# Another place modulo 512 bytes in SBUF for the activations of each chunk: windowed attention and a two-layer FFN on one core

## The chip, the cores and the metric

The kernel runs on one core of one Trainium2 chip. A core has five engines that run side by side: TensorE (PE: matmuls and transposes, results in PSUM; the loading of a matmul's stationary operand is shown apart as PEld), VectorE (DVE), ScalarE (ACT), GpSimd (POOL) and SyncE (SP, which here issues the DMAs). SBUF is the working memory on the chip, with 128 partitions; an address below is a byte address within a partition. The metric is the device time of the program in microseconds.

## The reference, cut to what matters

```python
# attention, batch 4, heads 8, seq 768, head_dim 64
k_sum = k.reshape(B, H, 24, 32, D).max(axis=3)
v_sum = v.reshape(B, H, 24, 32, D).mean(axis=3)
scores_l = scale * (q @ k.T)          # kept where |i - j| < 16
scores_s = scale * (q @ k_sum.T) + log(32)
a = softmax(concat(scores_l masked, scores_s))
attn = a @ concat(v, v_sum)
# feed-forward, 3072 tokens, d_model 512, d_ff 2048
x = attn.transpose(0, 2, 1, 3).reshape(3072, 512)
r = maximum(x @ w_in, 0)
out = (s * r * r + b) @ w_out
```

## The kernel before

The 3,072 tokens are worked on in 12 chunks of 256, c = 0 to 11 (three per batch entry); "chunk" below always counts from 0. For each chunk the attention of 4 pairs of heads gives x, kept transposed as 4 blocks (kc) of 128 features by 256 tokens. The feed-forward part then runs over 16 slices f of 128 hidden features:

- `hidden` (L364 in the trace) makes ph, 128 hidden features by 256 tokens: the stationary operand is a 128x128 block of w_in, the streamed one is x[:, kc], 256 columns. In chunks 1 to 11 the operands are split into a high and a low part (xh, xl and wh, wl, of type fp32r), and the sum has three products, w_l xh, w_h xl and w_h xh, over four kc: 12 matmuls per f, 192 per chunk. Chunk 0 uses plain fp32: 4 matmuls of the code per f, each of which is two instructions in the trace.
- `activate` makes g = s r^2 + b from ph: ACT (relu, square), POOL (scale and shift, L382), then DVE writes gh (L384) and gl (L386).
- `project` (L401) adds to po: the stationary operand is a block of 128 tokens of gh or gl, the streamed one is w_out (wh, wl), 512 columns. Two blocks of tokens by three products: 6 matmuls per f, 96 per chunk.
- `evict` copies po out and stores it.

So in `hidden` the activations are streamed and the weights are loaded, and in `project` it is the other way round. The weights of the next matmul are loaded while the present one streams.

The order of the work is written out by hand: `at(step, order, fn, ...)` files every piece under a step, two steps of f at a time; `project` of f comes two steps behind `activate` (LAG = 2), and the attention of chunk c + 1 (scores L266, transposes L314, values L334) is spread over the steps of chunk c. In chunk 11 there is no attention left to do.

Tiles come from pools, and a pool places its tiles one after the other. Weights lie in the pools `slots` and `wring`, whose tiles are 4,096 and 2,048 bytes; x, xh, xl, r, g, gh and gl are tags of the pool `p2`. In the built program of before every weight tile begins at 128 modulo 512, and every xh, xl, gh and gl of every chunk at 320 modulo 512, so that the two are 192 bytes apart in that measure. The blocks inside the tiles are 512, 1,024 or 2,048 bytes apart, so all operands of the fp32r matmuls begin at these two values.

Of the kernel before, what the change touches and what calls it, by code (L numbers as in the profile page):

```python
# [10 lines left out]
F32 = mybir.dt.float32  # L11
F32R = mybir.dt.float32r
# [6 lines left out]
P = 128  # L19
# [9 lines left out]
T = NSUB * SUB  # L29
# [4 lines left out]
NKC = DM // P  # L34
# [10 lines left out]
def windowed_attention_then_relu2_ffn(ctx, tc, qk, vwin, kt, vt, kq, vrow, wp, sb, out):  # L45


    nc = tc.nc
# [5 lines left out]
    p2 = ctx.enter_context(tc.tile_pool(name="p2", bufs=2))  # L54
# [160 lines left out]
    qk_t, vw_t, ps_of, pr_of, mn_of, sm_of, pt_of, pT_of, o_of, xt = ({} for _ in range(10))  # L215
# [107 lines left out]
    def values(c, p):  # L323
# [8 lines left out]
        for i in range(NSUB):  # L332
            for e in range(2):
# [2 lines left out]
                    vw[:, e, i, :], pT[:, e * T + i * SUB : e * T + (i + 1) * SUB], start=True, stop=True,  # L336
                )

    def attended(c, p):
        if p == 0:  # L340
            if c == 0:
                xt[c] = (p2.tile([P, NKC, T], F32, name="x", tag="xh"),)
            else:
                xt[c] = p2.tile([P, NKC, T], F32R, name="xh", tag="xh"), p2.tile([P, NKC, T], F32R, name="xl")
        kcs = slice(p, p + (1 if c < 2 else 2))
        o = o_of.pop((c, p))[:, : (kcs.stop - p) * T].rearrange("p (k t) -> p k t", t=T)
        nc.scalar.copy(xt[c][0][:, kcs], o)
        if c > 0:
            nc.vector.tensor_tensor(xt[c][1][:, kcs], o, xt[c][0][:, kcs].bitcast(F32), ALU.subtract)
# [18 lines left out]
    def activate(c, f):  # L368
        ph = ph_of.pop((c, f))
        r = p2.tile([P, T], F32, name="r")  # L370
        nc.scalar.activation(r, ph, AF.Relu)  # L371
        nc.scalar.activation(r, r, AF.Square)  # L372
        if c == 0:
            g = p2.tile([P, T], F32, name="g0", tag="gh", bufs=4)
            if f < 2:
                nc.vector.tensor_scalar(g, r, s_col, b_col, ALU.mult, ALU.add)
            else:
                nc.scalar.activation(g, r, AF.Identity, bias=b_col, scale=s_col)  # L378
            gg[c, f] = (g,)
            return  # L380
        g = p2.tile([P, T], F32, name="g")
        nc.gpsimd.tensor_scalar(g, r, s_col, b_col, ALU.mult, ALU.add)  # L382
        gh = p2.tile([P, T], F32R, name="gh", tag="gh", bufs=4)
        nc.vector.tensor_copy(gh, g)  # L384
        gl = p2.tile([P, T], F32R, name="gl", bufs=4)
        nc.vector.tensor_tensor(gl, g, gh.bitcast(F32), ALU.subtract)  # L386
        gg[c, f] = gh, gl

# [61 lines left out]
    for c in range(1, NC):  # L450
        bi, ci = place(c)
        for p in range(NPAIR):
# [31 lines left out]
            if c < 2 or p % 2 == 0:  # L484
                at(xa, ATT, attended, c, p)
# [10 lines left out]
    for i in range(NC * NF):  # L496
        c, f = divmod(i, NF)

        at(i if c == 0 else i - i % 2, HID, hidden, c, f)
        at(i, CHAIN, activate, c, f)  # L500
        at(i + LAG if i + LAG < NF else (i + LAG) | 1, PROJ, project, c, f)
        if f == NF - 1:
            at((i + LAG) | 1, EVICT, evict, c)
# [59 lines left out]
```

## Time and profile before

| what | value |
|---|---|
| median of two runs | 649.12 us (649.11 to 649.12) |
| the profiled execution | 648.77 us |
| its span, from the first to the last instruction | 647.1 us |
| mean granted clock of TensorE | 0.997 |
| HBM read and written | 55.90 MB, 6.29 MB |

The most expensive groups of TensorE on the page:

```profile
L401 PE MATMUL po<-wh,gl 128*128 128x512 f32 x352 | 143.2, 407 | 0.0
L364 PE MATMUL ph<-xh,wl_in 128*128 128x256 f32 x704 | 110.9, 280 | 0.0
L364 PEld LDWEIGHTS ph<-xh,wl_in 128*128 128x128 f32 x704 | 100.2, 188 | 8.2 <-ACT r L372 0.5
```

A row gives line, engine, operation, result and operands, shape and count; behind the first bar the busy time in us and the mean duration of one in ns, behind the second the idle time of the engine just before. Matmuls are pipelined: one that is recorded with 407 ns begins while the one before it is still under way, so that what a matmul costs in a row of them is read from start to start.

### The profile page before, as it was taken

The numbers are of one execution on the slowest core, as the hardware profiler recorded it, in microseconds if no ns is written. First come the engines' busy times: TensorE is split into PE (matmuls) and PEld (weight loads), VectorE is DVE, ScalarE is ACT, GpSimd is POOL, SyncE is SP. The second block draws the span as 40 slices with busy tenths as digits, with TensorE's granted clock in tenths as the row PEclk, the third lists the DMA queues.
The fourth block names the chain that finished last, engine by engine and source line by source line (L and its number), as shares of the span: only waits on it lengthen the run. The fifth ranks groups of instructions, "written<-read, shape, count | busy, mean of one in ns | idle before, by whom it ended". The sixth has DMA issues, their size and how long they took to land.

```text
span 647.1 us, 13906 instructions
## 1 busy us (share of the span) xinstructions
PE 630.3 (97%) x5164; PEld 549.1 (85%) x5164; DVE 332.7 (51%) x1088; ACT 338.4 (52%) x986; POOL 153.8 (24%) x324
## 2 busy tenths in 40 slices
PE   6799999999999999999999999999999999999997
PEld 4566568989989899898999899898998989999996
DVE  5799988885443434356434434447443353342221
ACT  4899998845444435535435345444444444452322
POOL 3000004143133132232231331331322322312221
PEclk9999999999999999999999999999999999999999
DMA  9999405035203204124402301504420320100000
GB/s 323 386 383 355 131 1 187 1 102 191 72 1 104 72 2 139 49 84 141 141 1 63 115 2 34 153 23 132 146 66 2 105 72 2 57 3 1 33 2 33
DMA packets 25604, 63.25 MB, mean 98 GB/s; under 512 B 3968, under 2 KB 3968, under 8 KB 25536
## 3 DMA queue, kind: packets, MB, share of 16 engines
q1 hardware_dynamic: 25536, 62.36, 29.3%
q8 instruction: 41, 0.67, 0.4%
q14 instruction: 27, 0.22, 0.1%
HBM read 55.90 MB, written 6.29 MB: 96 GB/s over the span
## 4 chain that ended last, share of the span: by engine, by line
PE 86%; ACT 7%; DMA 4%; DVE 2%; issue 0%; SPq 0%; DVEq 0%
PE po L401 39%; PE ph L364 38%; PE pav L334 4%; PE ps L266 3%; PE pt L314 3%; DMA wraw<-in_wp_dram 3%; ACT wraw L116 2%; ACT wraw L117 2%; ACT g L378 1%; DMA kq<-in_kq_dram 1%; ACT pr L298 1%; ACT r L372 1%; ACT r L371 0%; DVE wf_out L134 0%; DVE wf_out L132 0%; DVE wf_in L132 0%
## 5 line engine op out<-in xcount | busy, mean ns | idle before, releaser
L382 POOL TENSOR_SCALAR g<-r,sb_col 128x256 f32<-128x256 f32 x176 | 101.7, 578 | 418.5 <-ACT r L372 322.0
L384 DVE CAST gh<-g 128x256 fp32r<-128x256 f32 x176 | 52.4, 298 | 269.9 <-POOL g L382 269.6
L371 ACT ACTIVATE r<-ph 128x256 f32<-128x256 f32 x192 | 73.4, 382 | 203.8 <-PE ph L364 203.2
L401 PE MATMUL po<-wh,gl 128*128 128x512 f32 x352 | 143.2, 407 | 0.0
L401 PE MATMUL po<-wh,gh 128*128 128x512 f32 x352 | 138.6, 394 | 0.0
L401 PE MATMUL po<-wl_out,gh 128*128 128x512 f32 x352 | 137.7, 391 | 0.0
L364 PE MATMUL ph<-xh,wl_in 128*128 128x256 f32 x704 | 110.9, 280 | 0.0
L364 PE MATMUL ph<-xl,wh 128*128 128x256 f32 x704 | 108.7, 276 | 0.0
L364 PE MATMUL ph<-xh,wh 128*128 128x256 f32 x704 | 108.7, 276 | 0.0
L364 PEld LDWEIGHTS ph<-xh,wl_in 128*128 128x128 f32 x704 | 100.2, 188 | 8.2 <-ACT r L372 0.5
L364 PEld LDWEIGHTS ph<-xl,wh 128*128 128x128 f32 x704 | 93.8, 188 | 0.0
L364 PEld LDWEIGHTS ph<-xh,wh 128*128 128x128 f32 x704 | 92.9, 188 | 0.0
L372 ACT ACTIVATE r<-r 128x256 f32<-128x256 f32 x192 | 80.4, 419 | 6.1
L386 DVE TENSOR_TENSOR gl<-g,gh 128x256 fp32r<-128x256 f32 x176 | 76.4, 434 | 6.0
L401 PEld LDWEIGHTS po<-wh,gh 128*128 128x128 f32 x352 | 66.1, 188 | 14.3
L401 PEld LDWEIGHTS po<-wh,gl 128*128 128x128 f32 x352 | 66.2, 188 | 14.1 <-issue 3.0
L401 PEld LDWEIGHTS po<-wl_out,gh 128*128 128x128 f32 x352 | 66.3, 188 | 11.5
L298 ACT ACTIVATE pr<-pr,mn 128x120 f32<-128x120 f32 x176 | 67.4, 386 | 3.5 <-DVE mn L285 3.3
L321 ACT COPY pT<-pt 120x512 f32<-120x512 f32 x48 | 28.2, 587 | 37.0 <-PE pt L314 36.8
L364 PEld LDWEIGHTS ph<-x,wf_in 128*128 128x128 f32 x128 | 25.0, 200 | 14.3 <-issue 2.6
L244 POOL COPY vw<-vsum 24x256 f32<-24x256 f32 x80 | 36.8, 500 | 1.3
L308 DVE TENSOR_TENSOR pr<-pr,rs 128x480 f32<-128x480 f32 x48 | 35.4, 737 | 1.7
(71 smaller groups left out, 615.6 us busy)
## 6 DMA issues: line engine op xcount, KB each, us to landing
wraw<-in_wp_dram SPq DMA_DIRECT2D x32, 512.0 KB, 10.0
qk<-in_qk_dram SPq DMA_DIRECT2D x44, 368.0 KB, 4.7
vw<-in_vwin_dram SPq DMA_DIRECT2D x48, 192.0 KB, 4.2
out_dram<-o SPq DMA_DIRECT2D x24, 256.0 KB, 2.0
kraw<-in_kt_dram SPq DMA_DIRECT2D x12, 384.0 KB, 3.4
vraw<-in_vt_dram SPq DMA_DIRECT2D x12, 252.0 KB, 4.7
kq<-in_kq_dram SPq DMA_DIRECT2D x4, 512.0 KB, 4.6
vraw<-in_vt_dram SPq DMA_DIRECT2D x6, 264.0 KB, 7.0
```

The source lines that it names most:

```text
L244: filler(c).tensor_copy(vw_t[c, p][WIN:KR, e], vsum[bi][WIN : WIN + NB, 2 * p + e, :].unsqueeze(1).to_broadcast([NB, NSUB, D]),)
L298: nc.scalar.activation(pr, pr, AF.Exp, bias=mn_of[c, p][:, n : n + 1], scale=-1.0, accum_out=sm_of[c, p][:, n : n + 1])
L308: nc.vector.tensor_tensor(pr, pr, rs.unsqueeze(2).to_broadcast([P, 4, KR]), ALU.mult)
L321: nc.scalar.copy(pT_of[c, p], pt_of.pop((c, p))[:KR])
L334: nc.tensor.matmul(o[64 * e : 64 * e + 64, i * SUB : (i + 1) * SUB], vw[:, e, i, :], pT[:, e * T + i * SUB : e * T + (i + 1) * SUB], start ...
L364: nc.tensor.matmul(ph, w[:, kc * P : (kc + 1) * P], x[:, kc], start=(n == 0), stop=(n == len(terms) - 1))
L371: nc.scalar.activation(r, ph, AF.Relu)
L372: nc.scalar.activation(r, r, AF.Square)
L382: nc.gpsimd.tensor_scalar(g, r, s_col, b_col, ALU.mult, ALU.add)
L384: nc.vector.tensor_copy(gh, g)
L386: nc.vector.tensor_tensor(gl, g, gh.bitcast(F32), ALU.subtract)
L401: nc.tensor.matmul(po[t], a[:, t * P : (t + 1) * P], w, start=(f == 0 and n == 0), stop=(f == NF - 1 and n == len(terms) - 1),)
```

## The change

The tiles of xh, xl, gh and gl (and of x and g in chunk 0, which share their buffers) get 128 floats more, 512 bytes per block of buffers, and the kernel uses a part of them that begins `shift(c)` floats into the tile. Chunks 0 and 1 stay where they were, chunks 2 to 8 begin 64 bytes further modulo 512 with each chunk, and chunks 9, 10 and 11 lie at 32, 160 and 288 bytes from where chunk 1 lies. To make room, the scratch area for DMA descriptors at the start of SBUF is 2,048 bytes in place of 16,384.

```diff
+    def shift(c):
+
+        return 16 * (c - 1) if 1 <= c <= 8 else (0, 8, 40, 72)[c - 8] if c > 8 else 0
+
     def attended(c, p):
         if p == 0:
+            room = [P, NKC * T + 128]
             if c == 0:
-                xt[c] = (p2.tile([P, NKC, T], F32, name="x", tag="xh"),)
+                both = (p2.tile(room, F32, name="x", tag="xh"),)
             else:
-                xt[c] = p2.tile([P, NKC, T], F32R, name="xh", tag="xh"), p2.tile([P, NKC, T], F32R, name="xl")
+                both = p2.tile(room, F32R, name="xh", tag="xh"), p2.tile(room, F32R, name="xl")
+            xt[c] = [t[:, shift(c) : shift(c) + NKC * T].rearrange("p (k t) -> p k t", t=T) for t in both]
...
-            g = p2.tile([P, T], F32, name="g0", tag="gh", bufs=4)
+            g = p2.tile([P, T + 128], F32, name="g0", tag="gh", bufs=4)[:, :T]
...
-        gh = p2.tile([P, T], F32R, name="gh", tag="gh", bufs=4)
+        gh, gl = p2.tile([P, T + 128], F32R, name="gh", tag="gh", bufs=4), p2.tile([P, T + 128], F32R, name="gl", bufs=4)
+        gh, gl = gh[:, shift(c) : shift(c) + T], gl[:, shift(c) : shift(c) + T]
         nc.vector.tensor_copy(gh, g)
-        gl = p2.tile([P, T], F32R, name="gl", bufs=4)
...
-    nc = _bacc.Bacc("TRN2", target_bir_lowering=False, num_devices=1)
+    nc = _bacc.Bacc("TRN2", target_bir_lowering=False, num_devices=1, dynamic_dma_scratch_size=2048)
```

In the built program the instructions of every engine stand in the same order, with the same waits, as before. The operands lie so (bytes modulo 512; "distance" is the place of x and g minus that of the weights, modulo 512):

| chunk c | 0, 1 | 2 | 3 | 4 | 5 | 6 | 7 | 8 | 9 | 10 | 11 |
|---|---|---|---|---|---|---|---|---|---|---|---|
| x, g before | 320 | 320 | 320 | 320 | 320 | 320 | 320 | 320 | 320 | 320 | 320 |
| x, g after | 320 | 384 | 448 | 0 | 64 | 128 | 192 | 256 | 352 | 480 | 96 |
| weights, both | 128 | 128 | 128 | 128 | 128 | 128 | 128 | 128 | 128 | 128 | 128 |
| distance after | 192 | 256 | 320 | 384 | 448 | 0 | 64 | 128 | 224 | 352 | 480 |

All other tiles keep their place modulo 512; their addresses move by multiples of 512.

## The prediction

> **What bounds the kernel now.** I read the page's first parts, then the waits of TensorE, then windows cut at the chunks, then the order of time inside one chunk, and last the chain. The page:
>
> ```profile
> span 647.1 us, 13906 instructions
> PE 630.3 (97%) x5164; PEld 549.1 (85%) x5164; DVE 332.7 (51%) x1088; ACT 338.4 (52%) x986; POOL 153.8 (24%) x324
> PEclk9999999999999999999999999999999999999999
> ```
>
> PE is busy for 97% of the span, at the full granted clock in every slice. The waits of PE alone (who, for whom: total us, times, longest):
>
> ```profile
> PE ps L269 <- DMA kq<-in_kq_dram: 4.7, 1, 4.7
> PE ph L364 <- DVE wf_in L134: 2.7, 3, 1.9
> ...
> PE ps L270 <- DVE ksum L159: 0.4, 1, 0.4
> ```
>
> That is nine kinds of wait with about 13 us in all, and they lie ahead of the steady part. To see the steady part I cut windows at the first `hidden` matmul of c = 1, 2, ... 11 (window: its length, PE busy with its matmul count, clock, DMA share, GB/s):
>
> ```profile
> 99.33:150.79 51.46, 51.46 (x438) 1.00 0.36 104
> 150.79:201.08 50.29, 50.29 (x434) 1.00 0.22 72
> 201.08:251.37 50.29, 50.29 (x434) 1.00 0.17 58
> 251.37:301.67 50.30, 50.30 (x434) 1.00 0.35 107
> ...
> 502.84:553.14 50.30, 50.30 (x434) 1.00 0.18 58
> 553.14:602.47 49.33, 49.33 (x402) 1.00 0.06 20
> 602.47:647.07 44.60, 40.91 (x262) 1.00 0.07 24
> ```
>
> Two things are to be seen. PE never idles from chunk 1 to chunk 10. And the chunks 2 to 9 take the same 50.29 to 50.30 us, whatever the DMA does beside them (58 to 107 GB/s): in this stretch the time is the number of matmuls times the spacing of their starts, and nothing else. So only a change of that spacing can move the end.
>
> The spacing is read where no attention work lies between, in the last chunk (start us, us, engine line op, count of merged instructions):
>
> ```profile
> 632.23 0.39 PE L401 MATMUL po<-wh,gl 128*128 128x512 f32 x1
> 632.46 0.39 PE L401 MATMUL po<-wl_out,gh 128*128 128x512 f32 x1
> ...
> 634.75 0.39 PE L401 MATMUL po<-wh,gh 128*128 128x512 f32 x1
> 634.98 0.64 PE L364 MATMUL ph<-xh,wl_in 128*128 128x256 f32 x4
> 635.45 0.62 PE L364 MATMUL ph<-xl,wh 128*128 128x256 f32 x4
> 635.91 0.62 PE L364 MATMUL ph<-xh,wh 128*128 128x256 f32 x4
> 636.36 0.62 PE L364 MATMUL ph<-xh,wl_in 128*128 128x256 f32 x4
> 636.82 0.62 PE L364 MATMUL ph<-xl,wh 128*128 128x256 f32 x4
> 637.27 0.62 PE L364 MATMUL ph<-xh,wh 128*128 128x256 f32 x4
> 637.72 0.39 PE L401 MATMUL po<-wh,gl 128*128 128x512 f32 x1
> ```
>
> The durations (0.39, 0.62) overlap, so I use starts. Twelve matmuls of `project` (L401, w streams, g is the loaded weight) go from 632.23 to 634.98: 2.75 / 12 = 229 ns each. Twenty-four of `hidden` (L364, x streams, w is loaded) go from 634.98 to 637.72: 114 ns each; the settled fours take 0.45 (113 ns), the first four after a `project` 0.47 (118 ns).
>
> Chunk 0 streams the same shapes as plain fp32, where each matmul of the code is two instructions in the trace. The order of time, and then four pieces of the chain (start us, us, what):
>
> ```profile
> 54.79 1.89 PE L364 MATMUL ph<-x,wf_in 128*128 128x256 f32 x8
> 56.52 0.60 PE L314 MATMUL pt<-ident,pr 128*120 128x128 f32 x4
> ```
>
> ```profile
> 96.69 3.43 PE po L401 x8
> ...
> 134.49 2.77 PE po L401 x12
> 142.06 2.95 PE po L401 x12
> ...
> 637.88 5.51 PE po L401 x24
> ```
>
> There 256 columns take (56.52 - 54.79) / 8 = 216 ns and 512 columns 3.43 / 8 = 429 ns, nearly the same time per column. One fp32r instruction does its columns in about half of it, but not quite: 113 against 216 / 2 = 108, and 229 against 429 / 2 = 214.5. The fp32r matmuls lose 5 and 14.5 ns each, about 5 and 7%, to something that the slower fp32 ones don't show. The only difference that I can name is that they take their columns twice as fast from SBUF. This loss is what the change can touch.
>
> **The change, part by part.** It adds, removes and moves no instruction: on every engine the same instructions stand in the same order with the same waits. What differs is addresses. (Positions below are byte addresses modulo 512 in the built program, in the table of the section on the change.)
>
> The smaller DMA scratch and the larger buffers shift whole pools by multiples of 512 bytes; no DMA is issued by POOL's queue, whose scratch it is. Cost: 0, hidden by nothing since nothing is executed; the trace has no second placement to bound it, and all its rows have one.
>
> Padding of the tiles: same elements are read and written. Cost 0.
>
> The writers: ACT writes xh, DVE writes xl, gh and gl at the new places, in chunks 9 to 11 at an odd multiple of 32 bytes.
>
> ```profile
> L384 DVE CAST gh<-g 128x256 fp32r<-128x256 f32 x176 | 52.4, 298 | 269.9 <-POOL g L382 269.6
> L386 DVE TENSOR_TENSOR gl<-g,gh 128x256 fp32r<-128x256 f32 x176 | 76.4, 434 | 6.0
> ```
>
> If an odd place doubled both, each step of f (50.29 / 16 = 3.14 us) would hold 0.73 us more of DVE work, and DVE is busy 51% of the span by the page. `project` runs two steps behind `activate`, so this is covered by PE's own queue; without that cover it would be 0.73 x 48 = 35 us in the three chunks. I take 0.
>
> The readers are the term that counts. Chunks 2 to 11 are moved: ten chunks with 192 matmuls of `hidden` and 96 of `project` each, 1,920 and 960. Chunk 0 and chunk 1 keep 320. In `hidden` the x columns are streamed while the next w is loaded, in `project` w is streamed while the next g is loaded; the change alters the distance between the two reads from 192 bytes to every multiple of 64 modulo 512, and in three chunks to 224, 352 and 480.
>
> What do rows say of another distance? Two kinds of neighbours have distance 0 already. The last matmul of each `hidden` run streams xh at 320 while gl at 320 is loaded: the four from 637.27 to 637.72 take 0.45, as those before. The last `project` streams wh at 128 while wl_in at 128 is loaded: 634.75 to 634.98, 230 ns, as the rest. So distance 0 costs what distance 192 costs, within the 10 ns of these rows. The other distances have no row. They are bounded from both sides:
>
> - Below: the loss goes away and the spacing becomes half of the fp32 rows. 1,920 x 5 + 960 x 14.5 = 9.6 + 13.9 = 23.5 us gained, 625.6 us.
> - Above: each `hidden` costs 118 ns as the first four after a `project` do (+5), and each `project` what the runs of twelve behind a transpose cost, 2.95 against 2.77 (+15 ns, though a part of that is the change from fp32 to fp32r). 1,920 x 5 + 960 x 15 = 9.6 + 14.4 = 24 us lost, 673 us.
>
> I take 0, by the distance-0 rows, which are the nearest: same engine, same operands, same loop, only another distance. Even with one pair of distances the spacing of `project` wanders, 2.77 / 12 = 231 and 5.51 / 24 = 229.6; plus or minus 3 ns on 960 is about 3 us, and that is this case's own range, 646 to 652.
>
> A rule is to be weighed against these rows. The rows show fp32r at 113 and 229 ns, with a weight load beside every matmul. The Trainium skill, "TensorE: Matmul & The Clock Gate", section "Step-by-step: what each phase is for", says that TensorE has two independent read ports to SBUF, so that loading the next weights takes no bandwidth from the running matmul; by it no distance costs anything and the sum is 0. The same page, section "Back-to-back issue gap", gives N / 2.4 + 2.5 ns, 109 and 216 ns here, and an estimate by that figure puts the loss at 4 x 1,920 + 13 x 960 ns, some 20 us, that the trace has and the page doesn't know. The fp32 rows agree with it, the fp32r rows don't, so the page cannot exclude that the two reads hinder each other.
>
> **The sum.** Profiled execution 648.8 us, of which the span is 647.1; plus 0 for scratch, padding, writers and readers. The median of the runs shown is 649.1, 0.3 above the profiled one. Forecast: 649 us.
>
> **The rivals.**
>
> 1. *The reads meet.* The streamed columns and the weights being loaded fall on the same part of SBUF in most new positions, and the stream stands still for it. The place is every L364 and L401 of chunks 2 to 11. For it speaks that the fp32r spacing is above half of the fp32 one, and that it isn't fixed: 118 and 113 with the same operands, 229 to 231. Against it speak the two rows at distance 0. With one of the ten chunks at distance 0 left out, the price above is 0.9 x 24 = 22 us: 671. It passes the 2% mark (13 us) where about 5.4 of the ten chunks pay in full. With two to five of them it ends between 653 and 661, within 2%.
> 2. *The present distance is a poor one.* Some of the new ones let the fp32r matmuls run at the fp32 rate per byte. For it speaks that the loss exists; against it that it is the same at 0 and 192. Half of the bound below: 12 us gained, 637. Over 2% it needs 5.5 of the ten chunks free of loss.
> 3. *The change isn't what it says*, because a tile is placed elsewhere than the source suggests. Against it: the operands' addresses in the built program move by just 64 bytes a chunk. If a writer were hindered instead (DVE, above) and its cover failed, three chunks would give 649 + 35 = 684; I give it no more than a part of the first rival's tail.
>
> **How the numbers follow.** No effect of position, 646 to 652: 47%. Reads that meet in some chunks, ending within 2%: 17%. The same in most chunks, over 2%: 24%. A gain within 2%: 7%, a gain over 2%: 5%. Faster is then 5%, within 2% is 47 + 17 + 7 = 71%, slower 24%; 2% is about what a measurement of this kernel can tell from no change. The range goes down to 640, which leaves out the larger part of the gains (some 7%), and up to 672, the first rival at the price of the rows; a price beyond the rows (8%) is left out. Together 15% is outside.
>
> **What the changed profile would show.** The window of chunk 1 should again be 51.46 us and serves as a control. If no position matters, the windows of chunks 2 to 9 are all 50.3. If the first rival holds, they differ from chunk to chunk, and within a chunk the fours of L364 rise over 0.45 or the twelves of L401 over 2.77, with PE still without a wait. If the second holds, some windows are under 50. If a writer is hindered, PE shows idle time ahead of L401 with DVE as releaser in the windows of chunks 9 to 11. The forecast is wrong if any window of chunks 2 to 9 is off by more than 0.6 us, since ten such chunks are 6 us; and the argument from distance 0 is wrong if chunk 6 (distance 0) is not at 50.3.

## The result, and the profile after

| | before | changed |
|---|---|---|
| median of two runs | 649.12 us | 658.84 us (658.74 to 658.93) |
| span of the profiled execution | 647.1 us | 657.2 us |
| mean granted clock of TensorE | 0.997 | 0.997 |

The changed kernel takes 1.015 times as long, with a 95% interval of 1.0106 to 1.0193: slower by 9.7 us, and still within 2%. The page of the changed kernel, first parts:

```profile
span 657.2 us, 13906 instructions
PE 640.9 (98%) x5164; PEld 557.0 (85%) x5164; DVE 332.5 (51%) x1088; ACT 337.9 (51%) x986; POOL 153.0 (23%) x324
```

The span is 10.1 us longer, and PE is busy 10.6 us longer (640.9 for 630.3), with the same 5,164 matmuls. The engines that write x and g are as busy as before (DVE 332.5 for 332.7, ACT 337.9 for 338.4). PE's waits, the first and the last of nine, are about those of before (12.7 us in all, for 13.2):

```profile
PE ps L269 <- DMA kq<-in_kq_dram: 4.3, 1, 4.3
...
PE pt L314 <- ACT pr L298: 0.4, 1, 0.4
```

The windows of the chunks 1 to 11, cut at the same places as before (length, PE busy, clock, DMA share, GB/s), show where the time came from. In both kernels these cuts lie some 6 us behind the first `hidden` matmul of a chunk, in its second run of `hidden`:

```profile
99.61:151.07 51.46, 51.46 (x438) 1.00 0.36 105
151.07:202.36 51.29, 51.29 (x435) 1.00 0.22 69
202.36:253.60 51.24, 51.24 (x434) 1.00 0.17 56
253.60:305.07 51.47, 51.47 (x435) 1.00 0.36 105
305.07:355.45 50.38, 50.38 (x434) 1.00 0.23 71
355.45:406.74 51.29, 51.29 (x435) 1.00 0.18 56
406.74:457.98 51.24, 51.24 (x434) 1.00 0.35 107
457.98:509.45 51.47, 51.47 (x434) 1.00 0.21 68
509.45:560.79 51.34, 51.34 (x434) 1.00 0.18 56
560.79:611.50 50.71, 50.71 (x403) 1.00 0.06 19
611.50:657.20 45.70, 42.00 (x262) 0.99 0.06 24
```

Against 50.29 us, the chunks 2, 3 and 4 cost 1.00, 0.95 and 1.18 us more; chunk 5 costs 0.09 more; and 6, 7, 8 repeat 2, 3, 4 to 0.01 us. The pattern returns after four steps of 64 bytes, so 256 bytes is the period, and of the multiples of 64 only distance 192 modulo 256 (chunks 1 and 5) is free. The three odd places cost 1.05, 1.38 (50.71 for 49.33) and 1.10 (45.70 for 44.60). The sum over ten chunks is 9.9 us. Counted from the first `hidden` matmul, chunks 2 to 10 have the same lengths to 0.01 us, chunk 11 costs 1.23 (51.78 for 50.55), and the sum is 10.0. PE has no idle time in the first ten windows, and in the last as much as before (3.7 us): the matmuls lie further apart. In chunk 6, with all distances 0, in order of time:

```profile
355.49 0.64 PE L370 MATMUL ph<-xl,wh 128*128 128x256 f32 x4
355.96 0.64 PE L370 MATMUL ph<-xh,wh 128*128 128x256 f32 x4
...
357.88 0.60 PE L314 MATMUL pt<-ident,pr 128*120 128x128 f32 x4
...
360.85 0.39 PE L407 MATMUL po<-wh,gh 128*128 128x512 f32 x1
361.08 0.64 PE L370 MATMUL ph<-xh,wl_in 128*128 128x256 f32 x4
```

From 355.49 to 357.88 are twenty matmuls of `hidden` (now L370), 2.39 us, 120 ns each where there were 113 to 114. The last `project` (L407) still takes 0.23.

Means worked out from the starts of all such neighbours in a chunk, in ns, first `hidden`, then `project` without the one behind attention work: before 114.3 and 229.7 in every chunk 2 to 9; changed, chunk 2 119.8 and 229.2, chunk 3 117.8 and 232.8, chunk 4 119.4 and 232.0. For chunk 3 that makes 192 x 3.5 + 96 x 3.1 ns = 0.97 us, of the 0.95 found.

### The profile page after: what moved, and what is told of

Same layout as the page of the kernel before. It is cut to its first block, busy times and chain, and to the rows that moved or that the text cites. A ratio compares the mean times of both kernels' runs of the same rounds, so it can differ in the third digit from the quotient of the medians.

```text
span 657.2 us, 13906 instructions
## 1 busy us (share of the span) xinstructions
PE 640.9 (98%) x5164; PEld 557.0 (85%) x5164; DVE 332.5 (51%) x1088; ACT 337.9 (51%) x986; POOL 153.0 (23%) x324
## 4 chain that ended last, share of the span: by engine, by line
PE 88%; ACT 7%; DVE 2%; DMA 1%; issue 1%; SPq 0%; DVEq 0%
PE po L407 39%; PE ph L370 38%; PE pav L334 4%; PE ps L266 3%; PE pt L314 3%; ACT wraw L116 2%; ACT wraw L117 2%; PE pm L202 1%; DMA vn<-in_vrow_dram 1%; ACT g L384 1%; ACT pr L298 1%; ACT r L378 1%; DVE wf_in L132 0%; ACT r L377 0%; DVE wf_out L134 0%
## 5 line engine op out<-in xcount | busy, mean ns | idle before, releaser
L407 PE MATMUL po<-wh,gl 128*128 128x512 f32 x352 | 144.2, 410 | 0.0
L407 PE MATMUL po<-wh,gh 128*128 128x512 f32 x352 | 138.7, 394 | 0.0
L407 PE MATMUL po<-wl_out,gh 128*128 128x512 f32 x352 | 138.4, 393 | 0.0
L370 PE MATMUL ph<-xh,wl_in 128*128 128x256 f32 x704 | 112.7, 282 | 0.0
L370 PE MATMUL ph<-xh,wh 128*128 128x256 f32 x704 | 111.8, 281 | 0.0
L370 PE MATMUL ph<-xl,wh 128*128 128x256 f32 x704 | 111.7, 281 | 0.0
L370 PEld LDWEIGHTS ph<-xh,wl_in 128*128 128x128 f32 x704 | 101.7, 188 | 8.3 <-ACT r L378 0.5
L370 PEld LDWEIGHTS ph<-xl,wh 128*128 128x128 f32 x704 | 95.7, 189 | 0.0
L370 PEld LDWEIGHTS ph<-xh,wh 128*128 128x128 f32 x704 | 95.6, 189 | 0.0
L407 PEld LDWEIGHTS po<-wh,gh 128*128 128x128 f32 x352 | 66.2, 188 | 15.5
L407 PEld LDWEIGHTS po<-wh,gl 128*128 128x128 f32 x352 | 66.3, 188 | 14.6 <-issue 3.0
L407 PEld LDWEIGHTS po<-wl_out,gh 128*128 128x128 f32 x352 | 66.4, 189 | 11.7
L370 PEld LDWEIGHTS ph<-x,wf_in 128*128 128x128 f32 x128 | 24.6, 197 | 14.8 <-ACT r L377 3.5
```

The costliest lines, as they stand in the source:

```text
L370: nc.tensor.matmul(ph, w[:, kc * P : (kc + 1) * P], x[:, kc], start=(n == 0), stop=(n == len(terms) - 1))
L407: nc.tensor.matmul(po[t], a[:, t * P : (t + 1) * P], w, start=(f == 0 and n == 0), stop=(f == NF - 1 and n == len(terms) - 1),)
```

## The experiments

The kernel before, run beside them, took between 648.6 and 649.7 us. Unless an interval stands there, each has one timed run; since the windows of a chunk agree to 0.01 us from chunk to chunk, the verdicts rest on them.

**Padding, scratch and the period** (e1_256).

```diff
-        return 16 * (c - 1) if 1 <= c <= 8 else (0, 8, 40, 72)[c - 8] if c > 8 else 0
+        return 64 if c > 1 else 0
```

> As the changed kernel, with the same padding and the small scratch, but x and g of chunks 2 to 11 all begin 256 bytes further. If the cost repeats every 256 bytes (as chunk 5, 256 bytes further, suggests with its 50.38 us), every window of chunks 2 to 9 is 50.3 to 50.4 us and the time is 649 to 650. If it repeats only every 512 bytes, or if the padding and the scratch cost something in themselves, the windows are 51.2 to 51.5 us as in chunks 2 to 4, and the time is 659 to 661.

648.89 us. Its windows, chunks 2 and 3:

```profile
144.94:195.23 50.29, 50.29 (x434) 1.00 0.27 85
195.23:245.52 50.29, 50.29 (x433) 1.00 0.18 58
```

So the larger tiles, the small scratch and the move of whole pools cost nothing, and 256 bytes further is the same place.

**Distance or place?** Everything 64 bytes further (e4_all_64), and the weights alone 64 bytes further (e5_w_alone; a small tile ahead of x gives the 64 bytes back).

```diff
-    mean4 = const.tile([P, KR + 20], F32, name="mean4")
+    mean4 = const.tile([P, KR + 20 + 16], F32, name="mean4")
...
-        rs = p2.tile([P, 4], F32, name="rs")
+        rs = p2.tile([P, 64], F32, name="rs")[:, :4]
```

The second pair of lines stands only in the run with the weights alone. Both runs have the small scratch too.

> The kernel before, with everything behind the constants 64 bytes further: weights at 192, x and g at 384, the distance stays 192. Theory 1 (the distance between the streamed operand and the weights counts, modulo 256): all windows as before, 50.3 us, time 649. Theory 2 (the place of the activations alone counts, and only 64 modulo 256 is free): all eleven chunks pay as chunks 2 and 6 did, 51.3 us, time 660.

> The kernel before, with the weights alone 64 bytes further: weights at 192, x and g at 320 as before, distance 128. Theory 1 (distance): chunks 1 to 11 all pay what chunks 4 and 8 of the changed kernel paid at distance 128 modulo 256, windows of 51.47 us, time about 649 + 11 x 1.18 = 662. Theory 2 (place of the activations alone): nothing moves that counts, 649.

649.52 and 662.53 us. A window of the first, chunk 2, and then one of the second:

```profile
145.59:195.88 50.29, 50.29 (x434) 1.00 0.27 85
```

```profile
145.87:197.43 51.56, 51.56 (x434) 1.00 0.25 83
```

Moving both is free; moving the weights, with x and g where they always were, costs 1.27 us a chunk. The place of the activations alone is refuted: what counts is the distance between what is streamed and what is loaded.

**Which matmuls pay?** Only x moved by 192 bytes (e2_x_alone), then only g (e3_g_alone), chunks 2 to 11.

```diff
-        return 16 * (c - 1) if 1 <= c <= 8 else (0, 8, 40, 72)[c - 8] if c > 8 else 0
+        return 48 if c > 1 else 0
...
-        gh, gl = gh[:, shift(c) : shift(c) + T], gl[:, shift(c) : shift(c) + T]
+        gh, gl = gh[:, :T], gl[:, :T]
```

(With g alone the slice of x loses its shift instead.)

> As the changed kernel, but only xh and xl are moved, all by 192 bytes in chunks 2 to 11 (distance 128 in hidden, as in chunk 4), g stays at 320 (distance 192 in project). If the matmuls of hidden carry the cost, as their spacing of 118 to 120 ns in chunk 4 says, a window is 51.2 to 51.3 us, the time 658 to 659. If the cost is shared evenly with project, a window is 50.9 and the time 655.

> The counterpart of the run with x alone: only gh and gl are moved, by 192 bytes in chunks 2 to 11 (distance 128 in project), x stays (distance 192 in hidden). What chunk 4 of the changed kernel paid, 1.18 us, less what x alone paid, should be left: about 0.2 us a chunk, windows of 50.5 us, time 651 to 652. If the two are not additive (the cost needs both), the time is 649 or 658.

658.30 and 651.35 us. Chunk 4 of the run with x alone, then of that with g alone:

```profile
247.47:298.67 51.20, 51.20 (x433) 1.00 0.29 92
```

```profile
245.71:296.26 50.55, 50.55 (x434) 1.00 0.30 93
```

0.90 us a chunk with x moved, 0.25 with g moved, 1.15 together, of the 1.18 that chunk 4 had with both. They add up, nearly, and `hidden` carries most of it: 0.90 of 1.15 here, and 0.67 of 0.97 in chunk 3 by the spacings above.

**How wide is the free place?** (e6_fine)

```diff
-        return 16 * (c - 1) if 1 <= c <= 8 else (0, 8, 40, 72)[c - 8] if c > 8 else 0
+        return (0, 0, -1, 1, -2, 2, -4, 4, -8, -12, 12, -6)[c] % 128
```

> As the changed kernel, but x and g lie by small steps around the old place: chunk 2 -4 bytes, chunk 3 +4, chunk 4 -8, chunk 5 +8, chunk 6 -16, chunk 7 +16, chunk 8 -32, chunk 9 -48, chunk 10 +48, chunk 11 -24. If the streams meet in blocks of 64 bytes, distances of 192 to 255 should be alike and the plus side free; chunk 9 of the changed kernel (+32, 51.34 us) speaks against it. If the free place is a point, every chunk but those within a few bytes shows 51.2 to 51.5 us and the time is 656 to 660. If it is a stretch of some 16 bytes on both sides, chunks 2 to 5 are at 50.3, and the time is 653 to 655.

660.43 us. The windows of chunks 2 (-4 bytes), 3 (+4), 4 (-8), 5 (+8), then 10 (+48):

```profile
144.95:196.30 51.35, 51.35 (x434) 1.00 0.26 83
196.30:248.35 52.05, 52.05 (x434) 1.00 0.17 56
248.35:300.00 51.65, 51.65 (x434) 1.00 0.29 91
300.00:351.62 51.62, 51.62 (x434) 1.00 0.27 83
...
556.53:606.34 49.81, 49.81 (x402) 1.00 0.06 20
```

It is a point. Four bytes to either side already cost 1.06 and 1.76 us, more than most steps of 64.

**Matmuls alone** (e7_probe). The core of the kernel, after w and x are filled with a constant; each case is closed by two small fp32 matmuls as a mark:

```python
def hidden(s0, m0, count=96):      # s: weights, m: streamed, in bytes
    run([(s0 + 512 * (i % 4), m0 + 1024 * (i % 4)) for i in range(count)], 256)
    between()
```

> Nothing of the reference is computed: the kernel holds rows of matmuls alone, fp32r, 96 of 128x256 (hidden's shape) per case, with the streamed operand at distances 0, 16, ... 240 from the weights, then three cases at other absolute places, two where weights alternate so that only the load of the next or only that of the own weights stands at distance 192, eight cases of 48 of 128x512 (project's shape), and four in plain fp32. Theory 1 (the stream meets the load of the next weights): 113 ns at 192 and 117 to 120 elsewhere, at 192 again 113 whatever the absolute place; of the alternating cases the one with the next weights at 192 is at 113, the other at 117 to 120; plain fp32 is at 216 for a pair of instructions at all distances. If the own weights counted it would be the other of the two cases. If no case differs, the kernel's other engines are needed for the effect, and theory 1 falls.

In order of time, the 96 of a case merged (start, duration): distances 192 and 0, then a later 112 and 128, then distance 192 with the weights at 64, 512 columns at g's distance 0 and 32, and plain fp32 at distance 0:

```profile
26.06 11.17 PE L33 MATMUL acc<-xb,wb 128*128 128x256 f32 x96
...
37.54 11.78 PE L33 MATMUL acc<-xb,wb 128*128 128x256 f32 x96
...
121.33 11.18 PE L33 MATMUL acc<-xb,wb 128*128 128x256 f32 x96
...
132.82 11.66 PE L33 MATMUL acc<-xb,wb 128*128 128x256 f32 x96
...
227.60 11.16 PE L33 MATMUL acc<-xb,wb 128*128 128x256 f32 x96
...
286.18 11.16 PE L33 MATMUL acc<-xb,wb 128*128 128x512 f32 x48
...
297.64 11.46 PE L33 MATMUL acc<-xb,wb 128*128 128x512 f32 x48
...
379.83 10.63 PE L33 MATMUL acc<-plain 128*128 128x256 f32 x48
```

The effect needs no other engine: with TensorE alone, 96 matmuls take 11.17 us at distance 192 and 11.78 at 0, 6 ns each. From start to start, over the second half of a case, the trace gives 113.3 ns at 192, whatever the absolute place, and also at 112; elsewhere 116.7 to 120.0. These are the spacings of the kernel: 120.0, 117.8 and 118.8 at distances 0, 64 and 128, where chunks 2, 3 and 4 have 119.8, 117.8 and 119.4. For 512 columns it gives 226.7 at g's distance 0, 228.9 at 192, and 232 to 234 at the other six. Plain fp32 is at 215.8 per instruction (not per pair, as expected) at all four distances. The two alternating cases both gave 116.7: a good distance to the next weights alone, or to the own weights alone, does not free a matmul. So which load a stream meets isn't settled by this.

**All distances, smaller loads, bf16** (e9_probe). The same kernel with other cases.

> Nothing of the reference is computed: rows of matmuls alone again. 128x256 at all 64 distances that are a multiple of 4 bytes, then 128x512 likewise; then loads of only 32 or 64 columns, 128x128 matmuls, and bf16. If reads of 16-byte lines meet, distances that are no multiple of 16 cost as much as or more than their neighbours (the +4 and -4 chunks had 52.05 and 51.35 us) and 192 and 112 stay the only free ones. If the weight load is what disturbs the stream, a load of 32 columns disturbs it for a quarter of the time: 128x512 then costs clearly less than 229 ns at its poor distances, near 216. If the stream alone is slow, it stays at 226 or more. In bf16, with half the bytes, no distance should cost anything (near 109 and 216) if the bytes read per column are the cause.

At steps of 4 bytes, over the second half of a case, 256 columns: 113.3 ns at 192 and 112 alone, 116.7 to 123.3 at the other 62. 512 columns: 226.6 to 227.6 at seven of the 64 distances of g (0, 16, 100, 120, 132, 156, 240), 229 to 237 at the others, 4 and 252 among them. So no simple rule on 16-byte lines fits. The loads of 32 columns with 256 and with 512 streamed (distance 0), and bf16 with 256 and with 512:

```profile
714.74 3.82 PE L62 MATMUL acc<-xb,wb 128*32 128x256 f32 x32
...
731.35 7.60 PE L62 MATMUL acc<-xb,wb 128*32 128x512 f32 x32
...
834.99 5.41 PE L62 MATMUL acc<-bx,bw 128*128 128x256 bf16 x48
...
857.87 10.53 PE L62 MATMUL acc<-bx,bw 128*128 128x512 bf16 x48
```

With 512 columns a load of a quarter of the columns doesn't relieve the stream: 7.60 us for 32, from start to start 230 to 232 ns at all four distances, where near 216 was expected of a load that disturbs for as long as it lasts. With 256 columns it does: 113.3, 116.6, 113.4 and 113.3 ns at distances 0, 64, 128 and 192, where loads of 128 columns gave 120.0, 117.8, 118.7 and 113.3. So the size of the load counts for one shape and not for the other, and a loss in proportion to the load is not what the 512 columns show. In bf16 the spacing is 109.2 and 215.8 ns at all four distances tried. A bf16 column has half the bytes, but its loads are shorter too (98 ns in the trace, for 188 in fp32r), so these rows don't tell which of the two takes the effect away.

**A faster kernel?** g on the weights' place, distance 0, x at 192 (e8_g_on_w).

```diff
-        return 16 * (c - 1) if 1 <= c <= 8 else (0, 8, 40, 72)[c - 8] if c > 8 else 0
+        return 16 if c > 0 else 0
...
-            xt[c] = [t[:, shift(c) : shift(c) + NKC * T].rearrange("p (k t) -> p k t", t=T) for t in both]
+            xt[c] = [t[:, : NKC * T].rearrange("p (k t) -> p k t", t=T) for t in both]
```

> A try at a faster kernel: x stays at distance 192 from the weights, which is free in hidden, and g of chunks 1 to 11 goes to distance 0 modulo 256, where the rows of 128x512 alone ran at 226.7 ns, against 228.9 at 192. If project follows those rows, 96 x 2.2 ns = 0.21 us a chunk are gained and the time is about 647. If the twelve matmuls of a run are too few to settle, as in chunks 2 and 6 of the changed kernel, whose project ran at 229 to 230 with the same distance, the time is 649 to 650.

653.77 us, 1.007 times the kernel before (1.0054 to 1.0087). Neither guess holds. In order of time, chunk 3:

```profile
202.19 0.63 PE L370 MATMUL ph<-xl,wh 128*128 128x256 f32 x4
202.66 0.64 PE L370 MATMUL ph<-xh,wh 128*128 128x256 f32 x4
...
204.54 0.60 PE L314 MATMUL pt<-ident,pr 128*120 128x128 f32 x4
...
205.90 0.39 PE L407 MATMUL po<-wl_out,gh 128*128 128x512 f32 x1
...
207.49 0.39 PE L407 MATMUL po<-wh,gh 128*128 128x512 f32 x1
```

`project` does settle at 1.59 / 7 = 227 ns. But `hidden`, at its free distance of 192, now runs at 2.35 / 20 = 117.5, where the kernel before has 113: the same places modulo 512, another spacing. A hindrance by DVE, which writes g while `hidden` runs, would be a rival, but the settled `hidden` matmuls of chunks 2 to 9 are 117.8 ns apart both where a DVE instruction runs beside them (118) and where none does (1,034). So the distance doesn't fix the spacing alone; the state in which a run of matmuls is entered counts too.

**Ten pairs of places** (e10_places).

```diff
+    PLACES = {1: (192, 240), 2: (192, 16), 3: (192, 100), 4: (192, 120), 5: (192, 156), 6: (112, 0),
+              7: (112, 192), 8: (112, 240), 9: (112, 16), 10: (192, 132), 11: (112, 0)}
...
+        return (PLACES.get(c, (192, 192))[which] - 192) % 256 // 4
```

> A look for places that beat both kernels: in each chunk another pair (distance of x, distance of g), of places where rows of matmuls alone ran at 113.3 (x: 192, 112) or 226.7 ns (g: 0, 16, 100, 120, 132, 156, 240): chunk 1 (192, 240), 2 (192, 16), 3 (192, 100), 4 (192, 120), 5 (192, 156), 6 (112, 0), 7 (112, 192), 8 (112, 240), 9 (112, 16), 10 (192, 132), 11 (112, 0). If hidden and project each settle by their own distance, every window is some 0.2 us under the kernel before, 50.1 us in chunks 2 to 9, and the time about 647. If what counts is also the state in which hidden is entered, as the run with g on the weights' place suggests (project at 226.7, hidden stuck at 117 to 118), windows differ: 49.9 to 50.1 where both settle, 50.7 where hidden doesn't; the time is then 648 to 655.

653.00 us. Chunks 4 (192, 120) to 6 (112, 0):

```profile
246.69:297.44 50.75, 50.75 (x433) 1.00 0.31 92
297.44:348.66 51.22, 51.22 (x433) 1.00 0.28 84
348.66:399.14 50.48, 50.48 (x433) 1.00 0.18 57
```

No pair comes under 50.29. Where `project` settles at 227 (chunks 4 and 10), `hidden` at 192 has a median of 118, as in the run before. Two runs of `hidden` (now L373) in chunk 2, with the same places modulo 512:

```profile
145.55 0.62 PE L373 MATMUL ph<-xl,wh 128*128 128x256 f32 x4
146.00 0.62 PE L373 MATMUL ph<-xh,wh 128*128 128x256 f32 x4
...
151.02 0.63 PE L373 MATMUL ph<-xl,wh 128*128 128x256 f32 x4
151.49 0.63 PE L373 MATMUL ph<-xh,wh 128*128 128x256 f32 x4
```

The first settles at 113 ns (0.45 for four), the second at 118 (0.47). What ran before tells them apart, though not always. Behind a `project` that had settled at 227 every run of `hidden` at 192 went to 118, 21 here and 85 in the run before; behind one at 229, as in the kernel before, all 86 went to 113; behind one at 233 in this run eight went to 118 and four to 113. At 112 the runs behind 227 went to 113. No version was found that beats the kernel before.

## Why the prediction was wrong

**What bounds the kernel** was right. PE has no idle time in the steady part, its waits and the other engines' busy time hardly change, and the added time is spacing of matmuls. The windows of the prediction are not cut at the first `hidden` matmul, as it says, but some 6 us behind it; for the chunks 2 to 10 that changes no length by more than 0.01 us.

**The parts put at zero** for scratch, padding and writers were right: 648.89 us with all three and the distance kept; and matmuls alone, without a writer, show the effect.

**The readers, put at zero "by the distance-0 rows, which are the nearest",** is the step that failed: the term was put at 0 and measured 9.9 us. Chunk 6, named beforehand as its test, has distance 0 and took 51.29 us. The row of `hidden` was one matmul at the end of a run of twenty-four that had settled at distance 192, and one matmul doesn't show what a run of them settles to: 113 ns there, 120 in chunk 6. The row of `project`, one matmul too, came out right for `project`, whose spacing at distance 0 is as low as at 192 (229.2 and 229.7), but it said nothing of `hidden`. Two shapes were put into one argument, and the other distances, for which there was no row, were taken along at 0: they cost 0.95 to 1.38 us a chunk.

**The loss in the fp32r rows** was read rightly as the thing that the change can touch: plain fp32 and bf16, at the same columns, didn't depend on the four distances tried. The Trainium skill, "TensorE: Matmul & The Clock Gate", section "Step-by-step: what each phase is for", says that loading weights takes no read bandwidth from the running matmul; for bf16 and plain fp32 the runs agree at the four distances tried, for fp32r they don't (113.3 or 120.0 ns by distance alone). Its spacing of N / 2.4 + 2.5 ns ("Back-to-back issue gap", 109 and 216), which that section gives for an isolated matmul, is what a row of bf16 shows with 109.2 and 215.8; no fp32r row of 256 or 512 columns reaches it.

**The first rival was the mechanism,** in its milder form ("two to five of them ... between 653 and 661"; measured 658.8), though for another reason than given: not five chunks paid in full, but nine paid part; that the range fits is luck. Its price for `hidden`, +5 ns from the first four after a `project`, was good: 3.5 to 5.5 ns measured. The first four of a run in the kernel before are matmuls that haven't settled yet; at the other distances the whole run stays near their spacing (117.8 to 119.8 ns). Its price for `project`, +15 ns from the runs behind a transpose, was mis-sized: -0.5 to +4.3 ns measured. The run behind a transpose is longer for another reason than the distance, as suspected there: its first matmul is followed after 0.31 us at distance 192 and at distance 0 alike. With the right price, 0.7 to 1.1 us a chunk from `hidden` and up to 0.4 from `project`, nine chunks give the 9.8 us.

**The second rival,** a gain, falls for these places: 192 is one of the two best of 64 distances for `hidden`, and no pair tried with the seven better ones for `project` made a window shorter.

What remains open: why a column of fp32r costs 1/16 more than one of bf16 even at the best place (256 more columns of bf16 take 215.8 - 109.2 = 106.6 ns, and 113.3 is 17/16 of that), why the period is 256 bytes, why the size of the load counts for 256 columns only, and what decides at which spacing a run settles. That two reads of SBUF by TensorE hinder each other is argued from the dependence on distance; no run shows the memory itself.

## What to carry to other kernels

Where TensorE runs dense fp32r matmuls, the distance modulo 256 between the streamed operand and the weights is worth a probe: up to 9% of a 256-column matmul (113.3 to 123.3 ns) hang on it, to the exact 4 bytes, and a tile added ahead of a pool can change it unseen; with bf16 nothing hung on it at the four distances tried. Probe it in the kernel, not alone: the best place for each shape by itself made the kernel slower, because the spacing at which a run settles hangs on the run before it too. And a single neighbour in a trace with the wanted property is no evidence for a stream of them.

## What the runs showed of the hardware

- Matmuls at the same places modulo 512 settled at 113 or at 118 ns depending on what ran before. It is seen inside the changed kernel too: chunk 5 has the free distance, but its first run, entered from chunk 4, stays at 117 to 119 ns from start to start, and settles at 113 only in the second; counted from its first `hidden` matmul the chunk is 50.39 us, and that is its 0.09 us.
- Many spacings settle on round shares of the time that bf16 takes for as many columns more (106.6 ns for 256, 213.2 for 512, from the two bf16 rows): 113.3 and 120.0 ns are 17/16 and 18/16 of the one, 226.7 and 233.3 are 34/32 and 35/32 of the other.
- A 128x128 fp32r matmul takes 111.6 to 111.7 ns at all four distances tried, hardly less than 113.3 for twice the columns: the load of 128 weight columns may be the bound there, but no run tests it.
